# Copying attention's transposed output out of its bank once, and splitting it from SBUF on ScalarE and GpSimd

## The chip, the core and the metric

The kernel runs on one core of a Trainium2 chip. The metric is the device time of one execution in microseconds. A core has TensorE (PE in the profile, its weight loads PEld), VectorE (DVE), ScalarE (ACT), GpSimd (POOL) and SyncE (SP, which here issues nearly all DMAs). TensorE writes into PSUM banks; GpSimd has no access to them, so that what it works on must lie in SBUF.

## The reference, cut to what matters

One transformer block with adaptive layer norm, 2048 tokens of width 512, 32 heads of 16. Attention runs over four segments of 512 tokens, each with its own causal softmax and a read from a compressive memory. Then comes a gated bilinear layer.

```
x = A_x
h = layernorm(x) * (1 + ca) + sa
x = x + ga * attention(h)          # attention ends with  o @ wo
h = layernorm(x) * (1 + cb) + sb
x = x + gb * ((h @ w_gate) * (h @ w_up)) @ w_down
```

The change touches the step `o @ wo`: `o` is transposed on its way into the matmul, and both operands are fp32 values split into a high and a low part.

## The kernel before

A product of two fp32 matrices is made of three matmuls in a reduced fp32 format ("fp32r"): high x high, low x high, high x low. So each operand is needed as a pair, `xH` and `xL = x - xH`.

Attention is a written-out pipeline of 32 units (4 segments x 4 groups of 8 heads x 2 halves). In each of its slots PE makes logits twice: `q` (queries by keys, from which DVE takes the row maximum `nm` with a custom operation, in place in the bank) and `k` (keys by queries, from which ACT makes the exponentials `pt` and POOL masks the diagonal blocks). `tb` multiplies `pt` with the values, `tr` transposes the result back, and DVE divides it into rows `orow`, which go to DRAM (`od`).

Beside this pipeline the function `fill` puts other work into the slots, taken from two generators: `fill_a` (layer norm and projections of later segments) and, after it, `fill_b` (the output projection of earlier segments). PE's order is fixed by the order in which the program is written. The order on ACT and POOL comes from a scheduler; DVE's is chained in this part.

`fill_b` goes through segments 0, 1 and 2. Segment 3 is done after the last unit, in the main program. For each segment:

- `wo_load` brings the rows of `od` back into SBUF as `orl`;
- `wo_op` transposes them: for each of four groups, four PE transposes (L88) fill a bank `op`, ACT copies it to `oH` (L404), and DVE subtracts, `oL = op - oH` (the helper's line L39 in the profile);
- `wo_row` (through `wo_mm`) makes four output tiles `wops`, each of 4 groups x 3 matmuls, `woH` by `oH`, `woH` by `oL` and `woL` by `oH` (L85);
- `wo_add` adds the input rows `xr` on DVE and stores `x1d`.

In this part of the program the function `bank` hands out two PSUM banks in turn (tag `ms`), so that `op` of one group and `op` of the group after next, or `wops` behind them, share one. In segment 0 the weights are prepared beside it (`open_b`): `wor` is multiplied by a factor on POOL (L768), `woH` is made on ACT (L780), `woL` on POOL (L781) and DVE in turn. In segments 1 and 2 the layer norm of the gated layer (`lnC`, tiles `ctp`, `chf`, `chH`, `chL`) and the splitting of the gated layer's weights (`prep`) lie beside it.

After 540 us the gated layer follows (`gate_up`, L1014 and L1035), almost all of it on PE.

Of the kernel before, what the change touches and what calls it, by code (L numbers as in the profile page):

```python
# [8 lines left out]
F32 = mybir.dt.float32  # L9
F32R = mybir.dt.float32r  # L10
BF = mybir.dt.bfloat16
AF = mybir.ActivationFunctionType
# [5 lines left out]
P = 128  # L18
S, D, H, DH, NSEG, L, F = 2048, 512, 32, 16, 4, 512, 1376
# [38 lines left out]
def tile_kernel(ctx, tc, x, wq, wk_, wv, wo, beta, w_gate, w_up, w_down, c, w_mod, out):  # L58
    nc = tc.nc
# [19 lines left out]
    def pin(i):  # L79

        if last_pe[0] is not None:
            tc.add_manual_dep(i.ins, last_pe[0].ins.name, NOSYNC, reason="order")
# [4 lines left out]
    def TP(*a):  # L87
        return pe(nc.tensor.transpose(*a))  # L88

    CV, CA = Chain(tc, nc.vector), Chain(tc, nc.scalar)  # L90
    vec, act = Switch(nc.vector), Switch(nc.scalar)
    cst = ctx.enter_context(tc.tile_pool(name="cst", bufs=1))
    wpool = ctx.enter_context(tc.tile_pool(name="wp", bufs=1))
# [11 lines left out]
    def bank(name, dt=F32, shape=(P, 512)):  # L105

        nbank[0] += 1
        return pst(shape, btag[nbank[0] % len(btag)], name, dt)
# [284 lines left out]
    def wo_op(s, pb, rw, us, gs=range(NG)):  # L393

        for g in gs:
            op = bank(f"op{s}_{g}")
            for t in range(4):
                a = rw[t][:, g * P:(g + 1) * P]
                if s == NSEG - 1 and g == NG - 1:
                    a = orows[NSEG * NG - 1][:, t].rearrange("p h e -> p (h e)")  # L400
                TP(op[:, t * P:(t + 1) * P], a, ident)
            oH = pb.tile([P, L], F32R, tag="oH", name=f"oH{s}_{g}", bufs=6)
            oL = pb.tile([P, L], F32R, tag="oL", name=f"oL{s}_{g}", bufs=6)
            act.activation(oH, op, AF.Copy)  # L404
            us.append((oH, oL))
            yield 0.45
            pin(vec.tensor_sub(oL, op, oH.bitcast(F32)))
            if g % 2 == 1:
                yield False

# [429 lines left out]
    def fill_b():  # L840
        ob = open_b()
        next(ob)
        pb, bc = B["pb"], B["bc"]
        o1 = wo_load(1, pb)
        pr = prep(0, bc, pb, "cr", 3)
        next(pr)
        us = [[], [], []]
        yield from weave(wo_op(0, pb, B["orl"], us[0]), ob, (0, 1, 2, 3))
        while osegs[0] <= 2:
            yield None  # L850
        o2 = wo_load(2, wpool)
        yield from weave(wo_mm(0, us[0], pb), pr, (3, 6, 9, 12))
        yield from wo_op(1, pb, o1, us[1])
        pr = prep(1, bc, pb, "cr", 3)
        next(pr)
        lg = lnC(0, pb, bc, pb, "x1", 4)
        yield from weave(wo_mm(1, us[1], pb), lg, (1, 5, 6, 7, 8, 9, 11, 12, 13, 14))
        B["nxt"] = yield from lg
        yield from wo_op(2, pb, o2, us[2])
        B["orl_free"] = True  # L860
        yield from weave(wo_mm(2, us[2], pb), pr, (3, 6, 9, 12))
# [216 lines left out]
```

## Time and profile before

| | |
|---|---|
| median of 3 runs | 918.21 us (917.14 to 920.17) |
| profiled execution | 917.86 us, its span 916.1 us |
| busy: PE, DVE, ACT, POOL | 877.6, 534.9, 408.3, 315.5 us |
| `op` transposes | 418 to 536 us, 64 of them |
| `oH` on ACT, `oL` on DVE | 16 each, at 420.8 to 536.3 us |

The page gives busy times, a picture of the span in 40 slices, and the chain of work that ended last, followed back from the end. Other views give that chain in order of time, each engine's instructions in order of time with the idle time before each and what ended it (in brackets), and busy times in chosen windows with the clock that TensorE was granted (1.00 is full speed). Times in all of them are microseconds from the start of the span.

### The profile page before, as it was taken

What the parts mean: (1) busy time and instruction counts of PE and PEld (TensorE: products, weight loads), DVE (VectorE), ACT (ScalarE), POOL (GpSimd) and SP (SyncE); (2) the same over time, 40 slices, a digit from 0 to 9 for tenths busy, and PEclk for the clock granted to TensorE, in tenths of its full rate; (3) what the DMA queues carried; (4) which work ended last, traced back from release to release, by engine and by line L of the source; (5) the groups of instructions that cost most, each with busy time, mean ns of one, the idle gap of its engine ahead of it and who ended that gap; (6) DMA issues with size and microseconds to landing.
All of it is one profiled execution on the core that took longest, in us unless ns stands there. A gap on an engine that the chain in (4) does not pass through costs nothing.

```text
span 916.1 us, 14191 instructions
## 1 busy us (share of the span) xinstructions
PE 877.6 (96%) x5083; PEld 623.1 (68%) x5084; DVE 534.9 (58%) x1587; ACT 408.3 (45%) x603; POOL 315.5 (34%) x460
## 2 busy tenths in 40 slices
PE   8988999999999899998998999999999999999998
PEld 4655656556656565565655678887888788878886
DVE  8688877897789977787886326553133213321112
ACT  3647767787577865675546412231112111211111
POOL 4435536565464762666424406540000000000000
PEclk9989999999999999998998999999999999999999
DMA  7773544664455544659551433331101110100011
GB/s 230 223 215 115 186 117 155 205 197 145 134 164 178 179 133 125 198 181 307 169 170 59 139 126 109 110 95 58 46 1 47 47 47 0 47 19 29 1 46 47
DMA packets 86215, 109.81 MB, mean 120 GB/s; under 512 B 9504, under 2 KB 58656, under 8 KB 86144
## 3 DMA queue, kind: packets, MB, share of 16 engines
q1 hardware_dynamic: 86000, 108.89, 37.7%
q8 instruction: 40, 0.66, 0.3%
q14 instruction: 31, 0.25, 0.1%
q10 hardware_dynamic: 144, 0.02, 0.0%
HBM read 67.98 MB, written 40.63 MB: 119 GB/s over the span
## 4 chain that ended last, share of the span: by engine, by line
PE 59%; DVE 5%; ACT 3%; issue 1%; DMA 1%; POOL 0%; DVEq 0%
PE gps L1014 13%; PE acc L1035 13%; PE ups L1014 13%; PE wops L85 4%; PE tb L85 3%; PE k L85 3%; DVE q L39 3%; PE q L85 2%; PE qps L85 1%; PE vps L85 1%; ACT pt L296 1%; PE kps L85 1%; PE ctp L88 1%; PE tr L88 1%; PE up L85 1%
## 5 line engine op out<-in xcount | busy, mean ns | idle before, releaser
L39 DVE CUSTOM_DVE_ANT_0 q<-q,cmask 128x384 f32<-128x384 f32 (+3 forms) x512 | 246.9, 508 | 53.0 <-PE q L85 42.6
L296 ACT ACTIVATE pt<-k 128x1024 f32<-128x1024 f32 x160 | 163.7, 1023 | 77.3 <-PE k L85 75.5
L299 POOL TENSOR_SCALAR_AFFINE_SELECT pt<-pt 128x256 f32<-128x256 f32 (+1 forms) x224 | 99.4, 457 | 174.2 <-ACT pt L296 172.0
L1019 DVE TENSOR_TENSOR gs<-gs,ups 128x512 f32<-128x512 f32 (+1 forms) x44 | 30.2, 687 | 194.9 <-PE ups L1014 194.9
L85 PE MATMUL q<-kst,qst 96*128 96x384 bf16 (+3 forms) x512 | 101.6, 303 | 7.7 <-DVE nm L39 5.5
L85 PE MATMUL k<-qst,kst 98*128 98x384 bf16 (+3 forms) x512 | 98.4, 305 | 10.6 <-ACT pt L296 8.0
L1018 ACT ACTIVATE gs<-gps 128x512 f32<-128x512 f32 (+1 forms) x44 | 26.2, 597 | 146.6 <-PE gps L1014 146.6
L1022 ACT ACTIVATE mH<-gs 128x512 fp32r<-128x512 f32 (+1 forms) x44 | 27.8, 633 | 130.2 <-DVE gs L1019 126.7
L85 PE MATMUL tb<-pt,v 128*32 128x512 f32 (+3 forms) x1024 | 76.7, 440 | 0.0
L85 PEld LDWEIGHTS <-kst 98*128 98x128 bf16 x512 | 38.8, 99 | 53.6 <-issue 44.2
L39 DVE DVE_READ_ACCUMULATOR2_ANT nm<- 128x1 f32 x512 | 72.6, 142 | 0.0
L1014 PE MATMUL gps<-chH,gL 128*128 128x512 f32 (+1 forms) x176 | 69.3, 394 | 0.0
L1014 PE MATMUL gps<-chH,gH 128*128 128x512 f32 (+1 forms) x176 | 69.3, 394 | 0.0
L1014 PE MATMUL ups<-chH,uH 128*128 128x512 f32 (+1 forms) x176 | 69.3, 394 | 0.0
L1035 PE MATMUL acc<-dH,mL 128*128 128x512 f32 (+1 forms) x176 | 69.3, 394 | 0.0
L1035 PE MATMUL acc<-dL,mH 128*128 128x512 f32 (+1 forms) x176 | 69.2, 393 | 0.0
L1014 PE MATMUL gps<-chL,gH 128*128 128x512 f32 (+1 forms) x176 | 69.2, 393 | 0.0
L1014 PE MATMUL ups<-chL,uH 128*128 128x512 f32 (+1 forms) x176 | 69.2, 393 | 0.0
L1014 PE MATMUL ups<-chH,uL 128*128 128x512 f32 (+1 forms) x176 | 69.2, 393 | 0.0
L85 PEld LDWEIGHTS <-qst 96*128 96x128 bf16 x512 | 43.6, 98 | 35.2 <-issue 10.1
L1035 PE MATMUL acc<-dH,mH 128*128 128x512 f32 (+1 forms) x176 | 65.0, 395 | 0.0
L85 PEld LDWEIGHTS tb<-pt,v 128*32 128x32 f32 x1024 | 28.7, 110 | 39.9 <-issue 34.5
(215 smaller groups left out, 1660.7 us busy)
## 6 DMA issues: line engine op xcount, KB each, us to landing
kst<-kd SPq DMA_DIRECT2D x32, 384.0 KB, 4.4
qst<-qd SPq DMA_DIRECT2D x32, 384.0 KB, 5.2
wm<-in_w_mod_dram SPq DMA_DIRECT2D x24, 256.0 KB, 5.4
kd<-k SPq DMA_DIRECT2D x16, 384.0 KB, 4.0
qd<-q SPq DMA_DIRECT2D x16, 384.0 KB, 2.9
x<-in_x_dram SPq DMA_DIRECT2D x16, 256.0 KB, 4.2
kd<-k SPq DMA_DIRECT2D x16, 256.0 KB, 3.2
qd<-q SPq DMA_DIRECT2D x16, 256.0 KB, 3.4
```

The lines of the kernel that those rows point to most:

```text
L39: i = getattr(self.eng, name)(*a, **k)
L85: return pe(nc.tensor.matmul(*a, **k))
L88: return pe(nc.tensor.transpose(*a))
L296: act.activation(pt, kp, AF.Exp, scale=0.25)
L299: sels[u, i] = nc.gpsimd.affine_select(w, w, pattern=[[0, w.shape[1]], [1, P]], compare_op=ALU.is_ge, fill=0.0, base=0, channel_multiplier=-1)
L1014: nc.tensor.matmul(ps[0:n], a[:, k, 0:n], b[k], start=j == 0, stop=j == 11)
L1018: act.activation(gs[0:n], pss[0][0:n], AF.Copy)
L1019: vec.tensor_mul(gs[0:n], gs[0:n], pss[1][0:n])
L1022: act.activation(mH[0:n], gs[0:n], AF.Copy)
L1035: nc.tensor.matmul(acc[t], a[0:n, t * P:(t + 1) * P], b[0:n, :], start=i == 0 and j == 0, stop=i == NF - 1 and j == 2)
```

## The change

For segments 0, 1 and 2, ACT copies the bank once, as fp32, into a new SBUF tile `oF` (two buffers). From it ACT makes `oH`, and POOL makes `oL = oF - oH`. Segment 3 keeps the old way. `oH` and `oL` have five buffers each where they had six. The step of `wo_op` at which other work may come in between (`yield`) now stands behind the copy.

```diff
-            oH = pb.tile([P, L], F32R, tag="oH", name=f"oH{s}_{g}", bufs=6)
-            oL = pb.tile([P, L], F32R, tag="oL", name=f"oL{s}_{g}", bufs=6)
-            act.activation(oH, op, AF.Copy)
+            oH = pb.tile([P, L], F32R, tag="oH", name=f"oH{s}_{g}", bufs=5)
+            oL = pb.tile([P, L], F32R, tag="oL", name=f"oL{s}_{g}", bufs=5)
             us.append((oH, oL))
-            yield 0.45
-            pin(vec.tensor_sub(oL, op, oH.bitcast(F32)))
+            if s < NSEG - 1:
+                oF = wpool.tile([P, L], F32, tag="oF", name=f"oF{s}_{g}", bufs=2)
+                act.activation(oF, op, AF.Copy)
+                yield 0.45
+                pin(act.activation(oH, oF, AF.Copy))
+                nc.gpsimd.tensor_sub(oL, oF, oH.bitcast(F32))
+            else:
+                act.activation(oH, op, AF.Copy)
+                yield 0.45
+                pin(vec.tensor_sub(oL, op, oH.bitcast(F32)))
             if g % 2 == 1:
                 yield False
```

## The prediction

> **What bounds the kernel now.** I read the page's share of engines and its chain first, then the chain piece by piece where the diff works, then the engines one by one in those stretches.
>
> ```profile
> span 916.1 us, 14191 instructions
> PE 59%; DVE 5%; ACT 3%; issue 1%; DMA 1%; POOL 0%; DVEq 0%
> ```
>
> The second line is the chain that ended last, by engine: TensorE (PE) is the bound, and GpSimd (POOL) is nearly absent. So a change is worth what it gives to or takes from PE in its own stretch. The copies in question lie between 418 and 505 us, in three groups of four, one for each of segments 0, 1 and 2. The chain in order of time (start, length, what):
>
> ```profile
> 418.49 0.88 PE op L88 x8
> ...
> 423.70 0.68 DVE oL L39
> ...
> 426.26 0.61 DVE oL L39
> 426.91 6.40 PE wops L85 x15
> 433.31 0.45 PE k L85 x2
> ...
> 437.46 1.37 PE wops L85 x6
> ...
> 457.32 1.19 DVE oL L39 x2
> ...
> 460.78 2.29 PE tb L85 x32
> ...
> 504.64 0.70 DVE oL L39
> 505.39 3.69 PE wops L85 x15
> ...
> 509.08 0.45 PE k L85 x2
> ```
>
> The subtractions `oL` on VectorE (DVE) stand on the chain in all three segments, each time in front of the projection `wops`. PE's own timeline shows what its waits cost, in the brackets at the end:
>
> ```profile
> 422.14 0.66 PE L88 MATMUL op<-ident,orl 128*128 128x128 f32 x4 [1.03 <-DVE oL L39]
> 424.43 0.66 PE L88 MATMUL op<-ident,orl 128*128 128x128 f32 x4 [1.63 <-DVE oL L39]
> 426.91 0.79 PE L85 MATMUL wops<-woH,oH 128*128 128x512 f32 x1 [0.71 <-DVE oL L39]
> 457.98 1.25 PE L88 MATMUL op<-ident,orl 128*128 128x128 f32 x8 [0.79 <-DVE oL L39]
> ```
>
> The transposes `op` and the first `wops` use two banks in turn, so each waits until DVE has read the bank two places earlier. These are the stalls that an early copy of the bank would remove: 1.03 + 1.63 + 0.71 = 3.37 us in segment 0 and 0.79 us in segment 1.
>
> Last, the clock (eighth column of figures, PEclk) in chosen stretches:
>
> ```profile
> 426.90:432.60 5.70, 5.69 (x13) 4.45 (x14) 3.79 (x11) 0.85 (x1) 2.42 (x3) 0.50 1.08 366
> 490.40:495.30 4.90, 4.90 (x41) 1.72 (x38) 3.84 (x12) 2.41 (x4) 2.95 (x3) 0.65 0.15 55
> 500.60:504.50 3.90, 3.88 (x20) 3.48 (x21) 1.40 (x4) 2.73 (x4) 2.31 (x4) 0.56 0.75 246
> 437.10:438.60 1.50, 1.50 (x8) 1.11 (x6) 1.32 (x4) 1.05 (x2) 0.39 (x1) 1.00 0.82 254
> 456.00:461.00 5.00, 3.69 (x28) 2.25 (x30) 4.90 (x18) 3.66 (x5) 1.54 (x4) 1.00 0.72 203
> ```
>
> After PE's waits in segment 0 the granted clock is 0.50 for 5.70 us, although PE is busy: 15 `wops` take 6.40 us, 0.43 each, against 1.37 / 6 = 0.23 each at full clock. Two more such stretches follow, of 4.90 and 3.90 us.
>
> **The change part by part.** Twelve copies `oF` and twelve splits `oH` on ScalarE (ACT) take the place of twelve `oH`; twelve `oL` leave DVE for POOL. The order of the built program shows that PE and SP issue the same instructions in the same order as before, so no DMA is added or moved, and nothing after 545 us changes but its start.
>
> ```profile
> L39 DVE TENSOR_TENSOR oL<-op,oH x16: 677/685/692, 421.4 to 536.3; 128x512 fp32r<-128x512 f32 x16
> L404 ACT ACTIVATE oH<-op x16: 578/597/599, 420.8 to 535.7; 128x512 fp32r<-128x512 f32 x16
> L191 POOL TENSOR_TENSOR chL<-chf,chH 128x512 fp32r<-128x512 f32 x4 | 5.1, 1271 | 3.5 <-ACT chH L190 3.4
> ```
>
> DVE gives up 12 x 0.685 = 8.2 us. ACT gains 12 more operations of about 0.6, 7.2 us. POOL gains twelve subtractions; it has not done this one, but `chL` is the same form (two fp32 operands from SBUF, a split result): 1.27 us each, 15.3 us in all. That is nearly twice DVE's time, in a place where the result is wanted at once. There is a second, hidden wait: `oF` has two buffers, so the third copy of a segment waits in ACT's queue for POOL's first `oL`, the fourth for its second, and behind them queue the next `oH`, `woH` and the exponentials `pt`. The third and fourth bank are therefore freed at POOL's pace. `oH` and `oL` have five buffers for six, but the one reused is four or more groups old when it is wanted; I cost that at nothing, the cover being a whole segment's projection on PE.
>
> *Segment 0.* POOL already has work here, and DVE has two subtractions `woL`:
>
> ```profile
> 420.94 0.77 POOL L299 TENSOR_SCALAR_AFFINE_SELECT pt<-pt 128x256 f32<-128x256 f32 x2 [0.90 <-ACT pt L296]
> 421.96 1.27 POOL L781 TENSOR_TENSOR woL<-wor,woH 128x512 fp32r<-128x512 f32 x1 [0.25 <-ACT woH L780]
> 422.91 0.86 DVE L39 TENSOR_TENSOR woL<-wor,woH 128x512 fp32r<-128x512 f32 x1 [0.83 <-ACT woH L780]
> 423.66 2.51 POOL L768 TENSOR_TENSOR wor<-wor,gab 128x512 f32<-128x512 f32 x2 [0.44 <-DMA wor<-in_wo_dram]
> 426.12 1.28 POOL L781 TENSOR_TENSOR woL<-wor,woH 128x512 fp32r<-128x512 f32 x1
> 426.87 1.08 DVE L39 TENSOR_TENSOR woL<-wor,woH 128x512 fp32r<-128x512 f32 x1
> 427.82 0.63 POOL L299 TENSOR_SCALAR_AFFINE_SELECT pt<-pt 128x512 f32<-128x512 f32 x1 [0.42 <-ACT pt L296]
> 444.40 0.68 DVE L39 TENSOR_TENSOR crd<-crd,gbb 128x512 f32<-128x512 f32 x1
> 444.57 1.67 POOL L349 TENSOR_TENSOR orow<-orow,memb 128x512 f32<-128x512 f32 x1 [0.47 <-DVE orow L39]
> 504.19 1.28 POOL L349 TENSOR_TENSOR orow<-orow,memb 128x512 f32<-128x512 f32 x1
> ```
>
> POOL's new order is `woL`, `oL` 0, `wor`, `oL` 1, `wor`, the mask of `pt`, `oL` 2, `woL`, `oL` 3. It is free at 421.71 (420.94 + 0.77), and `woH` is there by then, since ACT now does it before `oH`. Eight operations at 1.27 and a mask at 0.63 are 10.8 us: `oL` 3 ends at 432.5. DVE and POOL also hold each other up when both work on two SBUF operands. DVE's `woL` end at 423.77 and 427.95, each 0.54 to 0.55 after POOL's own operation ended (423.23 and 427.40), and POOL's addition at 444.57 took 1.67 beside DVE's `crd`, against 1.28 alone at 504.19. With POOL in one unbroken row, each of the two DVE `woL` is let in between and costs POOL 0.55: 433.6. I take that; without it, 432.5.
>
> PE reaches `wops` sooner than now. The third copy `oF` runs when `oL` 0 is done (423.0 + 0.55 + 1.27, near 424.8) and takes 0.6, so the bank is free at 425.4 and not at 426.9. But then PE runs three matmuls and waits for `oL` 1, again for `oL` 2, again for `oL` 3. After the last come two matmuls of this row and three of the next before the next `k`. That `k` stands at 433.31 now. At 0.43 each it comes at 433.6 + 2.13 = 435.73, 2.42 later; at 0.23 each at 434.75, 1.44 later. Then the clock: between 427 and 433.6 PE would have some six matmuls, less than the idle stretch that led to the half clock before, so I expect it cold at 433.6 and cold for as long as the three stretches above, a mean of 4.8 us, to 438.4. Half of the 2.7 us behind 435.73 is lost: 1.3. Segment 0 costs 2.4 + 1.3 = 3.7 us, between 0.34 (POOL at 432.5, full clock) and 4.2 (5.7 us of half clock).
>
> The Trainium skill, "TensorE: Matmul & The Clock Gate", section "What's actually happening", states that a PE kept busy for a window of about 3.4 us gets its full clock. By that the cold stretch would end at 437.0, the segment cost 3.0 and the sum be 922.1 (an estimate from that page); the trace's 5.70 us of half clock on a busy PE is longer, so I stay with the rows.
>
> *Segment 1.* Here DVE has no gap from 453 to 460 and the two `oL` on the chain are 1.19 us of it. Without them the next reductions come 1.19 sooner, and with them PE's `q` and `tb`. PE idles 5.00 - 3.69 = 1.31 in the window from 456, so that is the most to gain. POOL has only short masks here, so two `oL` are done near 460, before `tb` ends at 461.9 (463.07 less 1.19) and the first `wops` wants them. ACT's added copies lie in its waits: it is busy 3.66 of those 5.00. Gain 1.2, between 0 and 1.3.
>
> *Segment 2.* DVE is hardly used here; what counts is again POOL.
>
> ```profile
> 500.60 0.63 ACT L190 ACTIVATE chH<-chf 128x512 fp32r<-128x512 f32 x1
> 501.45 0.60 ACT L404 ACTIVATE oH<-op 128x512 fp32r<-128x512 f32 x1 [0.23 <-PE op L88]
> ```
>
> The first split now takes the place of `chH` at 500.60 and ends at 501.23; `oF` 1 comes at 501.45, `chH` behind it ends near 502.58. POOL: `oL` 0 to 502.50, `chL` to 503.85, two masks (0.77) to 504.62, the addition `orow` (1.28) to 505.90, `oL` 1 to 507.17, `oL` 2 to 508.44, a mask to 509.07, `oL` 3 to 510.34. PE starts `wops` near 505.1, is held at each `oL`, and after the last has two and three matmuls: 510.34 + 1.15 = 511.49, against 509.08 for its next `k`. Cost 2.4, from 2.0 (chain start half a microsecond better) to 3.8 (matmuls at 0.43, 1.0 more, and one hold of 0.4 by DVE).
>
> By the Trainium skill, "SBUF — State Buffer", section "SBUF: two separate sides", an fp32 copy of DVE from SBUF to SBUF takes the ports it shares with GpSimd as well. The cast `gH` in this place would then cost POOL its 0.4 and the sum be 923.2; no row here shows a cast doing so, and I leave it in the upper bound.
>
> *Sum.* 3.7 - 1.2 + 2.4 = +4.9. The profiled execution took 917.86 us, its span 916.1 and 1.8 around it; the median of the three runs is 918.21, 0.35 above, and they spread from 917.14 to 920.17. So 917.86 + 4.9 = **922.8 us**. The bounds add to +1.0 (0.34 - 1.3 + 2.0) and +8.0 (4.2 - 0 + 3.8).
>
> **Rivals.** *Full clock* (0.19): the early start of `wops` and its scattered matmuls keep the clock up in segment 0. Then it is 1.44 - 1.2 + 2.4 = +2.6, 920.5, and without the holds between DVE and POOL 919.4, no change that can be told. For it: PE starts earlier; against it: the half clock came before with PE busier.
>
> *The bank wins* (0.07, the faster side): POOL keeps up, so that no `wops` waits for `oL`. The stalls of 3.37 and 1.2 in segment 1 go: 917.86 - 4.6 = 913.3. The point of decision is `oL` 3 of segment 0: PE would want it eleven matmuls behind 425.4, near 428.0, so POOL would have to do its eight operations and mask in 6.3 us, 0.7 each, DVE's speed. Every such row of POOL shows 1.27.
>
> *Cold twice* (0.13): the gaps that POOL leaves between PE's matmuls in segment 2 bring the half clock there too. Five matmuls cost 1.0 more and the tail 1.3: 4.2 - 1.2 + 2.4 + 2.3 = +7.7, 925.6. For it: the clock was already low at 500.60 to 504.50; against it: at half clock the matmuls nearly fill the gaps.
>
> **How the numbers follow.** My case has 0.61. A measurement here can tell about 0.3%, 2.75 us. Slower by more: 0.61 and 0.13, less a little for my case's low end, 0.73. Within: the full-clock rival and that low end, 0.20. Faster: 0.07. The range takes the bounds of the sum, 918.9 to 925.9, which leaves out the bank's win and the worst of the cold.
>
> **What would show it.** Right: `wops` waiting for POOL `oL` at L410, in segments 0 and 2 and not in 1; POOL without a gap from 421.7 to 433; `oL` at 1.27; ACT's `oF` waiting for POOL; the granted clock near 0.5 from before 433 to 437 or later; no `op` waiting for DVE. Wrong: if `oL` on POOL takes much under 1.27, if `wops` waits for something else, or if the clock is full at 434.

## The result and the profile after

The changed kernel takes 922.67 us (median of 11 runs, 919.88 to 926.84) against 918.21 us (11 runs) before: a ratio of 1.0045, with a 95% interval of 1.0028 to 1.0062. It is slower by 4.5 us; the prediction was 922.8. The profiled execution took 921.29 us, the third fastest of the eleven.

The page's first line and its chain that ended last, by engine:

```profile
span 919.6 us, 14203 instructions
PE 56%; DVE 5%; ACT 3%; POOL 2%; issue 1%; DMA 1%; SPq 1%; DVEq 0%; POOLq 0%; ACTq 0%
```

GpSimd (POOL) had 0% of the chain and has 2%: its pieces add up to 21.2 us where they were 3.8, and 7.6 of them are `oL`. Where it stands is told by the chain in order of time (start, length, what):

```profile
429.59 1.25 POOL oL L410
430.84 1.68 POOL woL L788
432.52 1.25 POOL oL L410
...
433.81 2.50 PE wops L85 x5
436.31 0.56 PE k L85 x2
...
462.68 2.29 PE tb L85 x32
...
506.50 2.50 POOL oL L410 x2
...
509.56 1.29 POOL oL L410
...
510.89 1.69 PE wops L85 x5
512.58 0.45 PE k L85 x2
```

In segments 0 and 2 the last `oL` of POOL now stands in front of the last five `wops`; in segment 1 it isn't on the chain. Ahead of 429.59 the chain leaves POOL for a load (`crg`) that an instruction in POOL's queue waited for; POOL itself has no gap there, as its timeline below shows. `k` of segment 0 came at 433.31 and comes at 436.31; the whole program already ran 0.60 us later at its first `op` (418.93 against 418.33 in TensorE's timeline), so 2.40 of the 3.00 us belong to the segment. TensorE's own timeline shows the three waits:

```profile
430.90 0.50 PE L85 MATMUL wops<-woH,oL 128*128 128x512 f32 x1 [1.41 <-POOL oL L410]
432.57 0.50 PE L85 MATMUL wops<-woL,oH 128*128 128x512 f32 x1 [1.17 <-POOL woL L788]
433.81 0.80 PE L85 MATMUL wops<-woH,oL 128*128 128x512 f32 x1 [0.36 <-POOL oL L410]
```

One of them waits for `woL`, which stands in the same row of POOL. The beginning and the end of that row, and the two VectorE (DVE) operations that get in its way:

```profile
422.37 1.27 POOL L788 TENSOR_TENSOR woL<-wor,woH 128x512 fp32r<-128x512 f32 x1
423.60 1.72 POOL L410 TENSOR_TENSOR oL<-oF,oH 128x512 fp32r<-128x512 f32 x1
...
430.81 1.71 POOL L788 TENSOR_TENSOR woL<-wor,woH 128x512 fp32r<-128x512 f32 x1
432.48 1.27 POOL L410 TENSOR_TENSOR oL<-oF,oH 128x512 fp32r<-128x512 f32 x1
```

```profile
423.16 1.04 DVE L39 TENSOR_TENSOR woL<-wor,woH 128x512 fp32r<-128x512 f32 x1 [2.32 <-ACT woH L787]
429.72 1.67 DVE L39 TENSOR_TENSOR woL<-wor,woH 128x512 fp32r<-128x512 f32 x1 [3.64 <-ACT woH L787]
```

From 422.37 to 433.75 POOL has no gap: 11.4 us. Two operations take 1.71 and 1.72 where the free one takes 1.27. Each of them began while a DVE `woL` was still running, which itself took 1.04 and 1.67. Both engines work on two fp32 operands from SBUF there. The new tile's rows, as the trace groups them, and the waits on POOL between 415 and 550 us (total, times, longest):

```profile
L407 ACT ACTIVATE oF<-op x12: 590/597/620, 419.6 to 507.8; 128x512 f32<-128x512 f32 x12
L409 ACT ACTIVATE oH<-oF x12: 621/632/652, 422.0 to 508.4; 128x512 fp32r<-128x512 f32 x12
L410 POOL TENSOR_TENSOR oL<-oF,oH x12: 1250/1276/1716, 423.6 to 509.6; 128x512 fp32r<-128x512 f32 x12
```

```profile
PE wops L85 <- POOL oL L410: 3.7, 4, 1.7
...
ACT oF L407 <- POOL oL L410: 2.9, 3, 1.5
...
PE wops L85 <- POOL woL L788: 1.2, 1, 1.2
```

`op` waits for DVE no more in segments 0 to 2 (one, in segment 2, waits 0.9 us for ACT's `oF` instead). No wait is for a buffer of `oH` or `oL`, which have five where they had six. Last the clock (the granted clock is the eighth column of figures). These windows are cut where the clock changes (but for the last one), the first two in the kernel before:

```profile
425.90:432.73 6.83, 6.12 (x16) 4.56 (x15) 4.78 (x13) 1.73 (x3) 3.42 (x4) 0.50 1.08 371
490.75:494.17 3.42, 3.42 (x17) 1.05 (x19) 2.77 (x11) 2.32 (x3) 2.08 (x3) 0.50 0.20 77
```

and these in the changed one:

```profile
426.17:429.58 3.41, 3.32 (x7) 1.69 (x7) 0.00 (x0) 2.77 (x5) 3.41 (x4) 0.50 1.10 358
429.58:433.00 3.42, 0.93 (x3) 0.48 (x3) 3.21 (x8) 0.11 (x1) 3.42 (x4) 1.00 1.05 384
433.00:436.41 3.41, 3.05 (x8) 1.67 (x7) 1.71 (x4) 0.00 (x0) 2.04 (x2) 0.50 1.06 347
436.41:439.80 3.39, 3.39 (x40) 1.44 (x39) 2.20 (x10) 1.16 (x2) 0.41 (x1) 1.00 0.77 218
508.09:511.50 3.41, 3.22 (x8) 1.69 (x8) 0.00 (x0) 0.94 (x2) 3.41 (x4) 0.50 0.10 27
490.60:495.10 4.50, 3.63 (x39) 1.97 (x43) 4.10 (x18) 3.51 (x5) 2.10 (x3) 1.00 0.15 58
```

Before, the clock was half for 6.83 us of segment 0. Now it is half for 3.41 us while TensorE runs its first `wops`, full for 3.42 in which TensorE mostly waits (the first busy figure, PE's, is 0.93), half again for 3.41 over the five `wops` behind the last `oL`, and full as soon as they are done. In segment 2 it is half until 511.50, over the first of the last five `wops`, which begin at 510.89. At 490.60 to 495.10, where before had a half clock from 490.75 to 494.17, it is full.

**The ledger of the two profiled executions.** TensorE issues the same instructions in the same order in both, so its start times can be set against each other. I cut at the first `op` of a segment and at the `tb` that follows its last `wops` before the next `k` (segments 0 and 2), or at the two `tb` around the transposes (segment 1). Differences, after less before: up to the first `op` +0.60, segment 0 +2.52, between -0.02, segment 1 -1.20, from there to segment 2 -1.19, segment 2 +2.79, the rest -0.07. They add up to +3.43, the spans' +3.5 within rounding. The +0.60 and the -1.19 lie where the change does nothing; the -1.19 goes with the clock that was low at 490 us in one run only. Without those two the change costs +4.0, near the medians' +4.5. The +0.60 is small of its kind: in the twelve profiles of this document the first `op` comes at 416.3 to 421.2 us, and no edit changes anything ahead of it. So a difference of two spans says little by itself.

### The profile page after: what moved, and what is told of

Read it like the earlier page. It is cut to its first block, busy times and chain, and to the rows that moved or that the text cites. A ratio compares the mean times of both kernels' runs of the same rounds, so it can differ in the third digit from the quotient of the medians.

```text
span 919.6 us, 14203 instructions
## 1 busy us (share of the span) xinstructions
PE 877.3 (95%) x5083; PEld 621.8 (68%) x5084; DVE 527.5 (57%) x1575; ACT 414.3 (45%) x615; POOL 332.2 (36%) x472
## 4 chain that ended last, share of the span: by engine, by line
PE 56%; DVE 5%; ACT 3%; POOL 2%; issue 1%; DMA 1%; SPq 1%; DVEq 0%; POOLq 0%; ACTq 0%
PE gps L1021 13%; PE acc L1042 13%; PE ups L1021 13%; PE wops L85 4%; PE tb L85 3%; DVE q L39 3%; PE k L85 3%; PE q L85 2%; PE qps L85 1%; PE vps L85 1%; ACT pt L296 1%; POOL oL L410 1%; PE ctp L88 1%; DMA crg<-in_w_gate_dram 1%; PE up L85 1%
```

## The experiments

The edits are to the changed kernel. Each time stands against runs of the kernel before on the same chip. S0, S1 and S2 are the lengths of the three stretches just defined, from the profiled execution of each kernel.

| kernel | S0 | S1 | S2 | median (before beside it) | ratio, 95% interval |
|---|---|---|---|---|---|
| before | 15.79 | 13.43 | 11.02 | 918.21 | |
| the change | 18.31 | 12.23 | 13.81 | 922.67 (918.21) | 1.0045 [1.0028, 1.0062] |
| segment 1 alone | 14.73 | 12.22 | 11.20 | 917.50 (918.77) | 0.9984 [0.9971, 0.9996] |
| the same again | 15.46 | 12.23 | 11.66 | 917.59 (918.13) | 0.9992 [0.9979, 1.0005] |
| segment 0 alone | 19.04 | 13.43 | 11.24 | 920.81 (918.50) | 1.0028 [1.0016, 1.0041] |
| segment 2 alone | 14.85 | 13.43 | 14.69 | 923.29 (918.50) | 1.0053 [1.0036, 1.0070] |
| `oL` from `oF` on DVE | 15.02 | 14.00 | 11.36 | 921.59 (918.77) | 1.0031 [1.0013, 1.0048] |
| the same, SP's order kept | 16.31 | 13.98 | 10.79 | 920.73 (918.50) | 1.0026 [1.0013, 1.0038] |
| four buffers of `oF` | 20.88 | 12.23 | 15.03 | 925.93 (918.77) | 1.0080 [1.0062, 1.0099] |
| all `woL` on DVE | 16.93 | 12.25 | 14.70 | 924.41 (918.77) | 1.0062 [1.0040, 1.0083] |
| DVE in 0, GpSimd in 1 | 15.51 | 12.23 | 11.33 | 916.87 (918.50) | 0.9991 [0.9977, 1.0005] |
| segment 1, all `woL` on GpSimd | 16.26 | 12.23 | 10.53 | 917.52 (918.13) | 0.9989 [0.9974, 1.0005] |

Each segment's length goes with the way it is done. With the old way S0 is 14.73 to 15.79 and S2 is 10.53 to 11.66; with the change's way S0 is 18.31 and 19.04 (20.88 and 16.93 where something else was edited too) and S2 is 13.81 to 15.03. S1 is 13.43 the old way and 12.22 to 12.25 with GpSimd.

**Segment 1 alone.** The new way is kept there; segments 0 and 2 go back to the old one.

```diff
-            if s < NSEG - 1:
+            if s in (1,):
```

> The new way in segment 1 alone; segments 0 and 2 as before. Three stretches are compared, each between two marks on TensorE: S0 from the first transpose `op` of segment 0 to the next `tb` (15.8 us before, 18.3 after the change), S1 from the `tb` ahead of segment 1's transposes to the `tb` behind them (13.4 and 12.2), S2 from the first `op` of segment 2 to the next `tb` (11.0 and 13.8). Theory (GpSimd's subtractions end last in segments 0 and 2 and are hidden in segment 1): S0 15.8, S1 12.2, S2 11.0, and the time 1.2 us below the kernel before, which is near the edge of what five rounds can tell. Rival (the doubled copies on ScalarE cost wherever they stand, and S1 was shorter only because its neighbours had moved): S1 13.4 or more, time 918 or above.

S1 is 12.22, shorter by 1.21, and the run 1.3 us faster than before. So the +4.5 lie in segments 0 and 2, and in segment 1 the step does gain what it takes off DVE. The same kernel was compared a second time:

> The kernel with the new way in segment 1 alone once more, beside the one above on the same chip, for a closer interval: S1 12.2, time 1.2 us below the kernel before if the gain is real, and within 0.3 of it if the first interval was luck.

S1 agrees to 0.01, the time is 0.5 us below before, between the two outcomes expected, and its interval takes in 1. A tenth of a per cent is as much as can be claimed. S0 shows why: the two profiles are of one and the same program, and differ by 0.73 in a stretch in which nothing is edited. In the windows view the first has its half clock at

```profile
421.47:428.30 6.83, 5.85 (x20) 4.53 (x21) 6.73 (x19) 2.76 (x4) 4.54 (x4) 0.50 0.99 329
```

and the second at

```profile
427.04:433.86 6.82, 6.53 (x20) 4.69 (x18) 5.52 (x16) 2.45 (x4) 3.95 (x4) 0.50 1.05 363
```

In the first it lies over the last transposes, `k` and `q`, and only the first half of the fifteen `wops`, which begin at 425.03; in the second it lies over the `wops` themselves, which begin at 428.81. The lengths S0 of the table are to be read with an uncertainty of about 1 us. The stretch behind S0 gives some of it back (13.58 and 13.15 us in these two).

**Segment 0 alone and segment 2 alone.** The same edit with `(0,)` and with `(2,)`.

> The new way in segment 0 alone. Theory: S0 17.3 to 19 (18.3 after the change, with a microsecond either way for the phase of the clock), S1 13.4, S2 11.0 to 11.4; time 2.5 us above before. Rival (the cost comes from all three together, through VectorE's and ScalarE's order): S0 below 17.

> The new way in segment 2 alone. Theory: S0 14.7 to 15.8, S1 13.4, S2 13.4 to 14.7; time 2.8 us above before. Rival (segment 2 lost only since the clock was low there): S2 11 to 12.

Segment 0 costs 2.3 us by the medians (920.81 - 918.50), segment 2 costs 4.8 (923.29 - 918.50) where 2.8 was expected. With segment 1 that is 2.3 - 1.3 + 4.8 = +5.8, against +4.5 measured for the whole. Segment 2 alone hit the half clock harder; its windows show

```profile
511.94:515.36 3.42, 3.42 (x15) 1.21 (x17) 1.02 (x2) 0.78 (x1) 0.77 (x1) 0.50 0.20 77
```

where the last four `wops`, `k` and the first part of `tb` lie.

**The subtraction back on DVE, but from `oF`.** This keeps ScalarE's (ACT) early copy and its doubled work, and takes POOL out of it.

```diff
-                nc.gpsimd.tensor_sub(oL, oF, oH.bitcast(F32))
+                pin(vec.tensor_sub(oL, oF, oH.bitcast(F32)))
```

> As after the change in all three segments, with `oF` and both copies on ScalarE, but `oL` is taken from `oF` by VectorE and not by GpSimd. Theory (GpSimd): S0 falls to 14 to 15.3 us, below the 15.8 of before, since the banks are free early and nothing waits for GpSimd's subtractions (VectorE's are held up now and then by GpSimd, as both read two SBUF operands); S1 13.2 to 13.4, the gain there gone, as VectorE has its work back; S2 10.5 to 11.2; time 916.5 to 918. Rival (ScalarE: twelve more copies, and `oF` ahead of the exponentials in its queue): S0 and S2 stay near 18 and 13, time 921 or more.

S0 and S2 fall back to 15.02 and 11.36, so ACT's copies are not what costs there. In segment 1 they do cost something once DVE has its subtraction back: S1 is 14.00, 0.57 above before, and DVE waits 0.46 us for ACT's `oH`, which comes behind the copy. Yet the time is 921.59. The profile shows something that I had not asked for: 19.08 us between segments 0 and 1 instead of 13.16. One row of DVE's waits and three of SyncE's (SP) timeline tell it:

```profile
DVE xr L39 <- DMA xr<-in_x_dram: 4.4, 1, 4.4
```

```profile
426.81 0.64 SPq L231 DMA_DIRECT2D kst<-kd  x1
428.00 2.55 SPq L389 DMA_DIRECT2D orl<-od  x4
431.10 4.21 SPq L422 DMA_DIRECT2D xr<-in_x_dram  x4
```

In the kernel before, SP's timeline has the load `xr` ahead of that load of `kst`:

```profile
427.67 2.77 SPq L415 DMA_DIRECT2D xr<-in_x_dram  x4
430.84 0.33 SPq L231 DMA_DIRECT2D kst<-kd  x1
```

The scheduler had moved `kst` forward, and `xr` came 3.4 us later in the queue; 1.2 of these are the later start of this run's first `op`, at 419.49. So the run is repeated with that order kept by a dependency without a wait, from the last load of `xr` to the load of `kst`:

```diff
+            if xrl[0] is not None and u == 29:
+                tc.add_manual_dep(i.ins, xrl[0].ins.name, NOSYNC, reason="order")
```

> The run with `oL` taken from `oF` by VectorE in all three segments, with one thing more: in that run one load of the keys, `kst`, had slipped ahead of the loads of `orl` and `xr` in SyncE's queue, and `xr` landed some 6 us later; an ordering dependency now keeps SyncE's order as it is before and after the change. Theory (GpSimd's time is the cost, and the 5.9 us lost between segments 0 and 1 in that run were the queue's): S0 near 15, the stretch between S0 and S1 back from 19.1 to 13.2, S1 13.4 to 14, S2 11.0 to 11.4, time within 1.5 us of before, so about 917 to 919. Rival (ScalarE's twelve extra copies cost it): the stretch between stays at 19, time 921 or more.

The gap is 13.16 again, so the queue's order had cost those 5.9 us. But the time, 920.73, is still 2.2 us above before, and S0 is no shorter than before's. This profile can't place all of the 2.2: of the 3.3 us that its span is longer than before's, 2.4 lie ahead of the first `op` (420.74 against 418.33), where nothing is edited, and the segments add 0.5, 0.55 and -0.2. DVE's timeline in segment 0:

```profile
424.45 1.55 DVE L39 TENSOR_TENSOR oL<-oF,oH 128x512 fp32r<-128x512 f32 x1 [1.81 <-ACT oH L412]
...
426.53 1.75 DVE L39 TENSOR_TENSOR oL<-oF,oH 128x512 fp32r<-128x512 f32 x1
...
430.08 1.71 DVE L39 TENSOR_TENSOR oL<-oF,oH 128x512 fp32r<-128x512 f32 x1
...
432.32 0.68 DVE L39 TENSOR_TENSOR oL<-oF,oH 128x512 fp32r<-128x512 f32 x1
```

and POOL's:

```profile
424.18 1.27 POOL L794 TENSOR_TENSOR woL<-wor,woH 128x512 fp32r<-128x512 f32 x1
...
426.30 3.10 POOL L781 TENSOR_TENSOR wor<-wor,gab 128x512 f32<-128x512 f32 x2 [0.84 <-DMA wor<-in_wo_dram]
...
429.96 1.28 POOL L794 TENSOR_TENSOR woL<-wor,woH 128x512 fp32r<-128x512 f32 x1
```

TensorE waits for what DVE has to do behind the second of these subtractions:

```profile
428.99 1.24 PE L85 MATMUL q<-kst,qst 96*128 96x384 bf16 x4 [4.17 <-DVE nm L39]
```

Three of the four subtractions take 1.55 to 1.75 beside an operation of POOL, the fourth 0.68. Before, with `op` read from the bank, the same subtraction took 0.677 to 0.692 all sixteen times, also beside the same POOL work (at 423.70 beside `wor`, at 426.18 beside `woL`). So neither theory holds as put: there is a third cost, that an `oL` taken from SBUF collides with POOL on whichever of the two engines it runs. The read of one operand from the bank had kept DVE out of POOL's way. S2, 10.79 and so no longer than before's 11.02 with all of ACT's copies in it, disposes of the rival that ACT is the price there. In segment 1, where none of the four `oL` on DVE is held (0.68 to 0.69 each), S1 is 13.98 and DVE again waits for ACT's `oH`, 0.47 us.

**Four buffers of `oF`.** This takes away ACT's wait for POOL (`oH` and `oL` get four too, for the room).

```diff
-                oF = wpool.tile([P, L], F32, tag="oF", name=f"oF{s}_{g}", bufs=2)
+                oF = wpool.tile([P, L], F32, tag="oF", name=f"oF{s}_{g}", bufs=4)
```

> As after the change, but `oF` has four buffers, so that no copy on ScalarE waits for GpSimd (`oH` and `oL` have four for five, to make room). Theory (GpSimd's row of subtractions): the waits of `oF` for `oL` (2.9 us in sum) go, but what TensorE waits for stays: S0 18.0 to 18.5, S2 13.5 to 14, time within 0.5 us of the change's. Rival (the wait of ScalarE's queue for a free `oF` holds up the splits, the exponentials and the bank): S0 near 16.9, S2 near 12.3, time 2.5 to 3 us below the change's.

No `oF` waits for POOL any more, and the kernel is slower still, by 7.2 us against before, which neither outcome had. The buffer was not the limit: POOL's row is as long as in the change, 11.4 us (424.96 to 436.33). It starts 4.45 us behind the first `op` instead of 3.44, because the scheduler placed `woH` later on ACT, and its last piece is now `woL`, for which seven matmuls wait and not five:

```profile
432.90 0.51 PE L85 MATMUL wops<-woH,oL 128*128 128x512 f32 x1 [1.22 <-POOL oL L410]
436.39 0.80 PE L85 MATMUL wops<-woL,oH 128*128 128x512 f32 x1 [2.99 <-POOL woL L788]
```

It is not a clean test of the wait alone, since the order moved with it; it does show that without that wait POOL's row still sets the end.

**All `woL` on DVE.** This takes two operations out of POOL's row.

```diff
-            (vec if k % 2 else nc.gpsimd).tensor_sub(woL[:, k, :], raws[k], woH[:, k, :].bitcast(F32))
+            vec.tensor_sub(woL[:, k, :], raws[k], woH[:, k, :].bitcast(F32))
```

> As after the change, but all four subtractions `woL` of the weights (beside segment 0) are on VectorE, two of them on GpSimd before. Theory (the length of GpSimd's row sets segment 0): the row is two operations of 1.27 us shorter, less what VectorE's own operations on two SBUF operands hold it up (0.55 each), so S0 falls by 1 to 1.6, to 16.7 to 17.3; S1 and S2 as after the change. Rival (segment 0 is set by something else, the clock or VectorE): S0 stays at 18.3 or grows.

POOL's last `oL` ends at 432.49 instead of 433.75, 1.26 sooner, and S0 is shorter by 1.38, as expected: the row sets the segment. The median of this kernel's four runs, 924.41, isn't lower than that of the change, though the two intervals overlap. Its profiled execution, at 921.22, was the fastest of the four, and it has 14.70 in S2, which the edit doesn't touch. Why the others were slower stays open.

**Two attempts at a better kernel.** In the first, segment 1 goes the new way, segment 0 has `oL` from `oF` on DVE with SP's order kept, and segment 2 is the old one. In the second, segment 1 alone goes the new way and all four `woL` are on POOL, so that DVE is free for `oL`.

> Each segment with what suits it: segment 0 takes `oL` from `oF` on VectorE, segment 1 as the change does it (GpSimd), segment 2 as before; SyncE's order kept as before. Theory: S0 near 15.0 (0.8 under before), the stretch to S1 13.2, S1 12.2, S2 11.0 to 11.2; time 1.2 to 2.5 us below the kernel before, 916 to 917. Rival (S0's 15.0 was only the clock's phase): the same as with segment 1 alone, 917.5.

> Segment 1 the new way; segments 0 and 2 as before, with VectorE's `oL` read from the bank; and the two `woL` that VectorE had beside segment 0 go to GpSimd. VectorE's own `woL` waited for GpSimd's operations there and stood in front of `oL`, the reader that frees the bank. Theory: in segment 0 GpSimd's row is woL, wor, woL, wor, woL, mask, woL, 6 x 1.27 + 0.63 and a wait for a load, from 422 to about 430.7 in the clock of before, ahead of the 433.3 at which the projection ends there; VectorE's `oL` come 0.9 to 2 us sooner; S0 14.2 to 15.6, S1 12.2, S2 11.0 to 11.4, time 916 to 917. Rival (the projection waits for GpSimd's last `woL`, as it did for `oL`): S0 15.8 to 17, time 917.5 to 919.

The first has S0 at 15.51, within the scatter of before's way (14.73 to 15.79). Three of its four `oL` again take 1.55 to 1.75. In the second, `op` waits 1.4 us for DVE instead of 2.7, and the projection waits for POOL's last `woL` in return, as the rival had it (S0 and the time lie in the rival's ranges):

```profile
428.28 0.50 PE L85 MATMUL wops<-woL,oH 128*128 128x512 f32 x1 [1.29 <-POOL woL L788]
...
430.11 0.79 PE L85 MATMUL wops<-woL,oH 128*128 128x512 f32 x1 [0.86 <-POOL woL L788]
```

By their ratios both are 0.1% below before (the first by 1.6 us in its median), with intervals that take in 1. No version's ratio is lower than the first one of segment 1 alone, and by the intervals the three can't be told apart.

## Why the prediction was right

**The mechanism.** Slower, because POOL's `oL` end last in segments 0 and 2 and the projection waits for them: that is what the chain shows, and what the segments done singly show (S0 and S2 grow only where the new way is in, S1 shrinks only there). Taking 1.26 us off the end of POOL's row took 1.38 off S0.

**Segment 0, the row of POOL.** Predicted to end at 433.6 with two holds of 0.55; with the program's 0.60 added, 434.2. It ended at 433.75, with two holds of 0.45 and 0.44. Without them it would have ended near 432.9 (433.75 - 0.89); the prediction's sum without holds gives 433.1 (432.5 + 0.60). `k` was expected 2.42 later and came 2.40 later. That agreement is luck, since two errors cancel: the row ended 0.45 sooner, and the five `wops` took 2.50 and not 2.13. I had not seen that a `wops` would wait 1.17 for `woL`; that changes nothing in the sum, since the `oL` behind it in the row ends later.

**Segment 0, the tail: the mis-sized term.** I took the half clock to begin at the last `oL`, to last 4.8 us (to 438.4 in the time of before), and to cost 1.3 more behind `k`. It began at 433.00, 0.76 us before the last `oL` was done, and lasted 3.41 us, to 436.41, 0.10 behind the start of `k` (436.31). So the segment cost 2.52 and not 3.7. The step that failed is "cold for as long as the three stretches above". Those 5.70, 4.90 and 3.90 us were the lengths of windows that I had cut, two of them with a mean clock of 0.65 and 0.56; the half clock in them lasted 6.83, 3.42 and 3.41 us. And TensorE ran its early `wops` at half clock while it had to wait for POOL anyway, had the full clock while it waited (429.58 to 433.00), and the half one again for the last five. The Trainium skill's window of about 3.4 us of work ("TensorE: Matmul & The Clock Gate", "What's actually happening"), from which the prediction had worked out 3.0 for this segment, came nearer than the rows that I preferred. The trace agrees with its length: 3.41 us here, and twice that in the kernel before.

**Segment 1.** Predicted -1.2, measured -1.20, and -1.20 or -1.21 where segment 1 went the new way alone. POOL's two late `oL` are hidden behind `tb` as expected, and in this stretch no `wops` waits for POOL.

**Segment 2.** Predicted +2.4, measured +2.79. POOL ended at 510.85, where the prediction with the offset of the two runs at that place (0.71, the ledger's first five terms) gives 511.05. The five `wops` behind it took 1.69 and not 1.15: the half clock of the rival *Cold twice* came, but it ended at 511.50, over the first of the five, and without its tail. The stretch done alone gave 4.8 by its medians, and S2 was 14.69 there, 15.03 with four buffers of `oF` and 14.70 with all `woL` on DVE; so how much the clock takes here changes from run to run, and the 13.81 of the change's profile is the least of the four. The row also has in it what the prediction left to its upper bound, a cast that collides with POOL. After, on DVE:

```profile
503.62 1.05 DVE L39 CAST gH<-crg 128x512 fp32r<-128x512 f32 x1
```

and on POOL at the same time:

```profile
503.11 1.28 POOL L191 TENSOR_TENSOR chL<-chf,chH 128x512 fp32r<-128x512 f32 x1
504.33 0.96 POOL L299 TENSOR_SCALAR_AFFINE_SELECT pt<-pt 128x256 f32<-128x256 f32 x2
```

Before, the same cast with POOL idle beside it:

```profile
505.96 0.42 DVE L39 CAST gH<-crg 128x512 fp32r<-128x512 f32 x1
```

The cast waits until POOL's `chL` is done (504.39) and ends 0.28 later, and the masks behind take 0.96 instead of 0.77. So the rule of the Trainium skill, "SBUF — State Buffer", "SBUF: two separate sides", that an fp32 copy between SBUF tiles takes the shared ports too, agrees with this trace; its price to POOL here was 0.2 and not the 0.4 that I had put in.

**The sum.** The terms give 2.5 - 1.2 + 2.8 = +4.1 against the predicted +4.9: segment 0 too dear by 1.2, segment 2 too cheap by 0.4. The median came 0.1 us from the forecast, closer than the terms were: that is luck.

**The rivals.** *Full clock* fell, by 0.50 behind the last `oL`. *The bank wins* fell: POOL's `oL` has a median of 1.276, and TensorE waits for it in segments 0 and 2. *Cold twice* is half true in the profile of the whole change, and segment 2 alone shows most of it. That `oF`'s two buffers would hold ACT was seen (2.9 us); four buffers gave nothing back, though that was not a clean test.

## What to carry to other kernels

What an operation's move is worth is decided by which queue ends last in front of its consumer: the same twelve subtractions, 0.69 us on DVE and 1.28 on POOL, gained 1.2 us in the segment where POOL's lateness was covered by other work and cost 2.5 and 2.8 in the two where TensorE wanted the result at once; such a change is best costed and switched place by place. Before an operand is moved from a PSUM bank to SBUF to free the bank, look at what the other of DVE and POOL does at that moment, because the read from the bank may have been what kept the two apart. And compare the DMA queue's order after every edit, even one that touches no DMA.

## What the runs showed of the hardware that was not expected

A subtraction of DVE with both fp32 operands in SBUF took 1.16 to 1.75 us beside an operation of POOL and 0.68 without, while the one with an operand in a bank kept to 0.69 beside the same work. An fp32 cast of one operand was held as well (1.05 against 0.42).

The half clock comes in steps of one length here. All 36 of its stretches between 415 and 530 us in the twelve profiles last 3.41 or 6.83 us. Where they fall moves from run to run of one program: the stretch from segment 1 to segment 2, in which TensorE does the same, took 37.7 us in the six profiles with a step of half clock in it and 36.5 in the six without.

The wait and its price stand in different steps. Cut each profile between 415 and 530 us into steps of 3.41 us, in phase with its own half clock. Behind all 26 steps of full clock in which TensorE was busy for 0.51 of the time or less, the next was at half clock; behind all 301 in which it was busy for 0.63 or more, the next was full; of the 17 between, some went one way and some the other. In the changed kernel TensorE was busy for 0.93 of 3.42 us from 429.58, at full clock, and paid for it in the step from 433.00. This is read from the traces, and no run tested it.
